# A linear-attention block with a gated feed-forward on one core: the statistics of the last two row tiles a pass sooner, one weight load later, and a finer row of opening products

## The chip, the core and the metric

The kernel runs on one core of a Trainium2 chip. The core has a matrix engine (TensorE, in the profile PE for the products and PEld for the loads of the stationary operand), a vector engine (DVE), a scalar engine (ACT), GpSimd (POOL) and a sync engine (SP) that here only issues DMAs. Every engine works through its own instructions in program order, and semaphores order the engines against each other. The metric is the device time of one execution in microseconds (us), lower is better.

## What is computed

Input x is 2048 rows of 640 numbers in bf16. There are 32 heads of 20 numbers. The reference, cut to what matters:

```python
def _A_ref(x, wqkv, w_phi, wo):                    # linear attention
    q, k, v = split of x @ wqkv into heads
    pq, pk = q @ w_phi[h], k @ w_phi[h]            # per head
    phi_q = concat(softmax(pq), softmax(-pq))
    phi_k = concat(softmax(pk), softmax(-pk))
    kv = sum over rows of phi_k^T v                # per head
    z  = sum over rows of phi_k
    o = (phi_q @ kv) / (phi_q @ z + 1e-6)
    return o @ wo
def _B_ref(x, w_gate, w_up, w_down):
    return (gelu(x @ w_gate) * (x @ w_up)) @ w_down
h   = x + _A_ref(layernorm(x), ...)
out = h + _B_ref(layernorm(h), ...)                # 640 -> 1536 -> 640
```

## The kernel before

The 2048 rows are 16 row tiles t = 0..15 of 128 rows, in four blocks of four tiles. All weights stay in SBUF. The order of the instructions on each engine is the order in which the Python text issues them; nothing reorders them, so a line's place in the text is its place in its engine's queue.

**Opening (L179 to L458).** SP loads x, W_v and the transposed W_k (`load_T(WkT, ...)`). While these are under way TensorE multiplies a constant tile by itself, `warm(*[512] * 7, *[P] * 8)` in L220: 15 products (7 of 512 columns, 8 of 128) whose result nothing reads. Each product in this kernel is a pair of TensorE instructions, a load of the stationary operand (PEld) and the product (PE). Then the first tiles are normalized and transposed by TensorE (`tp`), multiplied by W_v (`pv`), and w_phi is folded into W_k (`fold`, tile `wa`).

**The k pass (L463 to L511), one pass per tile t.** In this order: `k_tile(t)` multiplies tile t by the folded W_k (`pk`, ten products) and ACT writes two exponentials of it (`E`). In some passes `fold` multiplies a part of W_q (`wa`), or `kv_tile` adds phi_k^T v of earlier tiles into the accumulator `kvp` (40 small products per tile: tiles 0, 1 in pass 5; 2 to 5 in pass 9; 6 to 9 in pass 13). Then `v_mm(t + 4)` (`pv`, ten products), `ln_ap(t + 6)`, where ACT writes the normalized tile t + 6 (`ln`) and SP issues the DMA that transposes it into `LN1T`, and `v_ev(t + 4)`, where ACT evicts `pv` into `vS`. Then, in the passes 0, 2, 4 and 6, `ln_st(t + 8, t + 9)` (L485) takes the statistics of two tiles: four `bn_stats` and two `bn_aggr` on DVE (L114, L118), then on POOL variance plus eps (`ve`), its power of -1/2 (`rstd`) and two small scalings (`mr`, L132 to L138). Then `k_norm(t)`: DVE sums `E` (L325) and takes reciprocals (L329), and POOL and DVE write `vt` (L333). At the end of a pass SP may issue a transposing load of a part of W_q (`load_T(WqT, ...)`, passes 7 to 10); at the end of pass 13 it issues the loads of W_o and W_gate (L510, L511: 800 KB and 1920 KB).

**The q groups.** q is made transposed, in 13 groups `QG` of one or two 128x512 tiles: `q_mm(j)` does five products of 512 columns per tile into `pq`, `q_exp(j)` has ACT write two exponentials of it into `Eq[j]`. Pass 15, the last, holds groups 0 to 3: group 0, then `kv_tile` of tiles 10 to 12, then groups 1, 2 and 3. Behind the loop come `kv_tile` of 13 to 15 (L513) and `kv_mask`, where DVE evicts `kvp` into `KV`. Groups 4 and up lie in the text from L752 on, woven with the attention of tiles 0 to 2 (`attn_a`: small products `ab`). `load_late` (L525) loads W_up and W_down after group 4: a POOL copy of one column from `Eq[4]` into `Wu` (L527) makes the DMA behind it on SP (L528) wait for that group, and W_down's two DMAs follow on SP (L530).

**Feed-forward (from L813).** `gate_up` multiplies with W_gate and W_up (`gu`), ACT applies the gelu (`g`), DVE multiplies (`GT`), `down` multiplies with W_down (`pd`); the attention of the tiles 2 to 15 is woven in between. W_gate is first read by the first `gu` product.

PSUM holds four buffers of two banks (`gtile`) until `split`; `kvp` keeps one of them from pass 3 to `kv_mask`.

Of the kernel before, what the change touches and what calls it, by code (L numbers as in the profile page):

```python
# [17 lines left out]
def kernel(  # L18
# [12 lines left out]
    nc = tc.nc  # L31
    P = 128
# [5 lines left out]
    NT = S // P  # L38
# [23 lines left out]
    UH = H // 2  # L62
    QH, QF = H // 4, D // 4
    QUAD = [slice(32 * r, 32 * r + 32) for r in range(4)]

    SLOT = [(c, 3 * c // 2, 2) if c % 2 == 0 else (6 + 3 * (c // 2), 3 * (c // 2) + 1, 3) for c in range(NC)]
    SL = 12
# [16 lines left out]
    Wg = const.tile([P, NC, FF], BF16, name="Wg")  # L84
# [3 lines left out]
    Eq = [const.tile([P, len(g), 2, 512], BF16, name=f"Eq{j}") for j, g in enumerate(QG)]  # L88
# [15 lines left out]
    def gtile(name):  # L104
        return psG.tile([P, 2, 512], F32, name=name, tag="G")

    def ln_stats(pool, tiles, tag, act=True, between=None, log=False):

        n = len(tiles)
        mv = small(pool, [P, n, nc.vector.BN_AGGR_DIM], "mv" + tag)  # L110
        stats = small(pool, [P, n, 2, nc.vector.BN_STATS_DIM], "stats" + tag)
        for j, xt in enumerate(tiles):
            for i in range(2):
                nc.vector.bn_stats(stats[:, j, i, :], xt[:, i * HD:(i + 1) * HD])  # L114
                if between and i == j == 0:
                    between()
        for j in range(n):
            nc.vector.bn_aggr(mv[:, j, :], stats[:, j])  # L118
        ve = small(pool, [P, n], "ve" + tag)
        rstd = small(pool, [P, n], "rstd" + tag)  # L120
        if log is not False:

            def root():
                nc.scalar.activation(ve, mv[:, :, 1], ACTF.Ln, bias=eps)
                nc.scalar.activation(rstd, ve, ACTF.Exp, scale=-0.5)

            if log is True:
                root()
            else:
                log.append(root)  # L130
        else:
            nc.gpsimd.tensor_scalar_add(ve, mv[:, :, 1], EPS)  # L132
            nc.gpsimd.tensor_tensor(rstd, ve, nhalf[:, 0:n], op=ALU.pow)

        mr = small(pool, [P, n], "mr" + tag)
        if act:
            for j in range(n):
                nc.gpsimd.tensor_scalar(mr[:, j:j + 1], mv[:, j, 0:1], rstd[:, j:j + 1], -1.0,  # L138
                                        op0=ALU.mult, op1=ALU.mult)
        return [(xt, mv[:, j, 0:1], rstd[:, j:j + 1], mr[:, j:j + 1]) for j, xt in enumerate(tiles)]  # L140
# [58 lines left out]
    wg_v = B_w_gate.rearrange("(c p) n -> p c n", p=P)  # L199
# [16 lines left out]
    def warm(*cols):  # L216
        for n in cols:
            nc.tensor.matmul(wu[:, 0, 0:n], lhsT=ones[:, 0:P], rhs=ones[:, 0:n], start=True, stop=True)

    warm(*[512] * 7, *[P] * 8)  # L220

    def fold(WT, W2, quarters, ds=range(NC)):


        n, w = (2, QF) if quarters else (1, HD)
        runs = []
        for c in range(NC):
            lo, hi = H0[c] * Dh, (H0[c] + NH[c]) * Dh
            for r in range(2 * n):
                a, b = max(lo, r * w), min(hi, (r + 1) * w)  # L230
                if a < b:
                    runs.append((r // n, r, c, a, b))
        runs.sort()
        for d in ds:
            wa = gtile("wa")
            wr = wa.rearrange("p u (q x) -> p (u q) x", q=n)
            for i, (u, r, c, a, b) in enumerate(runs):
                nc.tensor.matmul(wr[:, r, a - r * w:b - r * w], lhsT=WT[:, c, d * P:(d + 1) * P],  # L238
                                 rhs=BD[:, c].rearrange("p a b -> p (a b)")[:, a - H0[c] * Dh:b - H0[c] * Dh],
                                 start=(i == 0 or runs[i - 1][0] != u),  # L240
                                 stop=(i + 1 == len(runs) or runs[i + 1][0] != u), skip_group_check=True)
            dst, src = W2[:, d, :].rearrange("p (u f) -> p u f", u=2), wr[:, :, 0:w]
            if quarters:
                dst = W2[:, d, :].rearrange("p (c r f) -> p r c f", c=NC, r=4)
                src = src.rearrange("p r (c f) -> p r c f", c=NC)
            if d in (QA if quarters else KA):
                nc.scalar.copy(dst, src)
            else:
                nc.vector.tensor_copy(dst, src)
# [15 lines left out]
    def ln_st(*tiles, act=True, between=None, log=False):  # L265
        for t, v in zip(tiles, ln_stats(p1, [x_sb[t // 4][:, t % 4, :] for t in tiles], "1", act, between, log)):
            lnp[t] = v

    def ln_ap(t, on_act=False, on_pe=False):
        ln = (ln_act if on_act else ln_dve)(p1, "1", *lnp[t])  # L270
        if on_pe:
            lnp[t] = ln
        else:
            transpose_to(LN1T[t // 4][:, :, t % 4 * P:(t % 4 + 1) * P], ln, False)
# [38 lines left out]
    def k_tile(t):  # L313
        pk = gtile("pk")
        proj(pk, t, Wk2, rows=t == 0)
        Ek[t] = ev.tile([P, 2, D], BF16, name="E", bufs=8)
        for s in range(2):
            nc.scalar.activation(Ek[t][:, s, :].rearrange("p (u f) -> p u f", u=2), pk[:, :, 0:HD],  # L318
                                 ACTF.Exp, scale=((lnp[t][2], nrstd[t]) if t in CT else (1.0, -1.0))[s])
# [25 lines left out]
    def kv_tile(t):  # L345

        for s in range(2):
            for c in range(NC):
                i, h, n = SLOT[c]
                for r in range(4):  # L350
                    f0, h0 = r * QF + c * 32, r * QH + h
                    nc.tensor.matmul(kvp[QUAD[r], s * SL + i:s * SL + i + n, :],  # L352
                                     lhsT=Ek[t][:, s, f0:f0 + 32], rhs=Vt[t][:, s, h0:h0 + n, :],
# [23 lines left out]
    def q_exp(j, signs=(0, 1)):  # L377
        for s in signs:
            nc.scalar.activation(Eq[j][:, :, s, :], pqs[j][:, 0:len(QG[j])], ACTF.Exp, scale=(1.0, -1.0)[s])  # L379
# [83 lines left out]
    for t in range(NT):  # L463
        if t == T3:
            kvp = gtile("kvp")[:, 0, 0:2 * SL * VC].rearrange("p (h f) -> p h f", f=VC)
        k_tile(t)
        if t == 0:
            ln_ap(6)
        if t in FQ:
            fold(WqT, Wq2, True, [i for i, f in enumerate(FQ) if f == t])  # L470
        for i in KVG.get(t, ()):
            kv_tile(i)
        for j in range(len(QT)):
            if t == QT[j]:
                q_mm(j)
                q_exp(j)
                for i in KVQ.get(j, ()):
                    kv_tile(i)
        if 0 < t < NT - 4:
            v_mm(t + 4)  # L480
        if t > 0 and t + 6 < NT:
            ln_ap(t + 6, on_act=True)
        if 0 < t < NT - 4:
            v_ev(t + 4)
        if t % 2 == 0 and t + 8 < NT:  # L485
            ln_st(t + 8, t + 9)
        k_norm(t)
        load_T(WqT, 0, *[i for i, f in enumerate(LQ) if f == t])
        if t == 10:
            transpose_to(LN1T[0][:, :, P:2 * P], ln_a(1), False)  # L490
        if t == 12:
            ln_ap(0, on_act=True)
        if t == 7:
            nc.gpsimd.memset(kmask[QUAD[0]], 1.0)
            for k, lo, n, base in ((3, 0, 2, 0), (2, 6, 3, 12)):
                m = kmask[QUAD[0], lo:lo + 6].rearrange("p (k n) -> p k n", k=k)
                nc.gpsimd.affine_select(out=m, in_=m, pattern=[[4, k], [-Dh, n]],
                                        compare_op=ALU.is_ge, fill=0.0, base=base, channel_multiplier=1)
                nc.gpsimd.affine_select(out=m, in_=m, pattern=[[-4, k], [Dh, n]],
                                        compare_op=ALU.is_ge, fill=0.0, base=Dh - 1 - base, channel_multiplier=-1)  # L500
        if t == 8:
            nc.gpsimd.memset(KV, 0.0)
        if t == 9:
            for r in (1, 2, 3):
                nc.sync.dma_start(kmask[QUAD[r]], kmask[QUAD[0]])
        if t == 11:
            nc.gpsimd.tensor_copy(KV[:, 0, :, KC - 1], kmask)
            nc.gpsimd.tensor_copy(KV[:, 1, :, 0], kmask)
        if t == 13:
            nc.sync.dma_start(Wo, wo_v)  # L510
            nc.sync.dma_start(Wg, wg_v)  # L511
    q = len(QT)
    for t in range(13, NT):  # L513
        kv_tile(t)
    kv_mask()
# [28 lines left out]
    def attn_a_mm(t):  # L544
# [9 lines left out]
        for s in range(2):  # L554
            for c in range(NC):
                i, h, n = SLOT[c]
                h += s * QH
                for r, q in enumerate(QUAD):
                    nc.tensor.matmul(ab[r][:, h * KC:(h + n) * KC], lhsT=eq(t, c, s)[q],  # L559
# [295 lines left out]
```

## Time and profile before

| | us |
|---|---|
| median of 3 runs (lowest, highest) | 277.1 (276.02, 277.8) |
| the profiled execution | 276.27 |
| its span, first to last instruction | 274.3 |
| TensorE busy in the span | 268.3 |
| DVE / ACT / POOL busy in the span | 174.2 / 141.0 / 96.3 |

All times inside the trace count from the span's start. The profiled execution's own time is 1.97 us above its span; that remainder lies before the first and after the last instruction. A row of the timeline gives start and length of a group of like instructions, the engine, the line, the operation and its tiles, and in brackets how long the engine had been idle before and what ended that. A matmul's length in the trace includes its latency, so that back-to-back products overlap in it: a 512-column product is listed with 379 ns, and the groups of twenty with 4.32 us, 0.216 us from start to start. "PEq", "SPq" and the like are an engine's sequencer, that is its instruction stream. "issue" means that the engine waited for nothing that the profile shows. In the part on the DMA queues q1 is the queue of the kernel's own DMAs, and q8 and q14 carry instructions.

### The profile page before, as it was taken

The page shows a single profiled execution, that of the slowest core. Times are in us where ns is not written, and L with a number is a line of the kernel's source. Part 1 is how long each engine was busy: PE and PEld are TensorE (multiplying, and loading weights), DVE is VectorE, ACT ScalarE, POOL GpSimd, SP SyncE. Part 2 cuts the span into 40 slices and gives each one's busy share as a digit, 9 for nine tenths or more (in the row PEclk, how much of TensorE's full clock was granted, in tenths as well). Part 3 has the DMA queues.
Part 4 walks back from the last instruction along what each step waited for, and adds up shares of the span by engine and source line. Part 5 has one row for each costly group of instructions (what it writes and reads, how often), then busy time and mean ns, then how long its engine had stood idle before and what let it go on. Part 6 is the DMA issues. An engine that isn't in the chain of part 4 may idle for free.

```text
span 274.3 us, 7230 instructions
## 1 busy us (share of the span) xinstructions
PE 268.3 (98%) x2978; PEld 171.8 (63%) x2995; DVE 174.2 (63%) x332; ACT 141.0 (51%) x241; POOL 96.3 (35%) x219
## 2 busy tenths in 40 slices
PE   8999999999999999999999999999999999999996
PEld 4777777764555887788754555675555576444574
DVE  5889999997585776775459863336976333333332
ACT  5789888786689755374534445212445510223100
POOL 4248899675002227374221552101165300000000
PEclk9999999999999999999999999999999999999999
DMA  7962527578078022323111232110214211000011
GB/s 204 215 225 56 75 51 98 75 149 312 2 264 310 5 50 43 79 54 71 38 38 49 26 72 50 45 53 1 68 30 62 37 48 50 24 0 0 2 48 48
DMA packets 42400, 21.46 MB, mean 78 GB/s; under 512 B 35200, under 2 KB 40576, under 8 KB 42368
## 3 DMA queue, kind: packets, MB, share of 16 engines
q1 hardware_dynamic: 41712, 20.98, 31.2%
q8 instruction: 23, 0.38, 0.6%
q10 hardware_dynamic: 656, 0.03, 0.2%
q14 instruction: 9, 0.07, 0.1%
HBM read 10.18 MB, written 2.62 MB: 47 GB/s over the span
## 4 chain that ended last, share of the span: by engine, by line
PE 90%; DMA 3%; ACT 2%; issue 1%; POOL 1%; DVE 1%; SPq 0%; ACTq 0%
PE gu L691 38%; PE pd L710 19%; PE po L631 8%; PE pq L374 8%; PE pk L285 6%; PE pv L285 5%; PE ab L559 2%; PE kvp L352 2%; DMA LN1T<-ln 2%; DMA Wv<-in_A_wqkv_dram 1%; PE wa L238 1%; ACT vS L305 1%; ACT ln L144 1%; PE tp L157 1%; PE pv L301 1%
## 5 line engine op out<-in xcount | busy, mean ns | idle before, releaser
L697 DVE TENSOR_TENSOR GT<-gu,g 128x512 bf16<-128x512 f32 (+1 forms) x60 | 34.5, 581 | 47.3 <-PE gu L691 38.5
L694 ACT ACTIVATE g<-gu 128x512 bf16<-128x512 f32 (+1 forms) x60 | 30.7, 512 | 63.7 <-PE gu L691 62.8
L691 PE MATMUL gu<-LN2T,Wg 128*128 128x512 bf16 (+1 forms) x289 | 61.2, 335 | 0.6
L691 PE MATMUL gu<-LN2T,Wu 128*128 128x512 bf16 (+1 forms) x300 | 61.7, 336 | 0.0
L710 PE MATMUL pd<-Wd,GT 128*128 128x320 bf16 (+2 forms) x396 | 53.5, 295 | 0.0
L710 PEld LDWEIGHTS <-GT 128*128 128x128 bf16 x396 | 37.9, 98 | 14.6 <-DVE GT L697 0.2
L691 PEld LDWEIGHTS <-Wu 128*128 128x128 bf16 x300 | 29.3, 98 | 22.6
L691 PEld LDWEIGHTS <-Wg 128*128 128x128 bf16 x300 | 28.6, 98 | 20.8
L285 PEld LDWEIGHTS <-LN1T 128*128 128x128 bf16 x290 | 27.8, 98 | 10.8 <-DMA LN1T<-ln 0.4
L713 DVE TENSOR_TENSOR y<-pd,x_sb 128x320 bf16<-128x320 f32 (+2 forms) x29 | 13.9, 480 | 29.4 <-PE pd L710 29.4
L333 POOL TENSOR_TENSOR vt<-vS,rs 128x672 bf16<-128x672 bf16 x22 | 29.2, 1346 | 7.6 <-DVE rs L329 7.2
L631 PE MATMUL po<-Wo,oT 128*128 128x320 bf16 x160 | 24.4, 299 | 0.0
L374 PE MATMUL pq<-LN1T,Wq 128*128 128x512 bf16 x94 | 23.1, 379 | 1.2 <-PE kvp L352 0.5
L285 PE MATMUL pk<-Wk,LN1T 128*128 128x320 bf16 x160 | 24.2, 299 | 0.0
L325 DVE TENSOR_REDUCE sk<-E 128x64 f32<-128x1280 bf16 x16 | 22.9, 1430 | 0.0
L379 ACT ACTIVATE Eq<-pq 128x1024 bf16<-128x1024 f32 (+1 forms) x26 | 20.0, 828 | 3.8 <-PE pq L374 3.8
L285 PE MATMUL pv<-Wv,LN1T 128*128 128x320 bf16 x130 | 19.8, 299 | 0.2 <-DMA LN1T<-ln 0.2
L631 PEld LDWEIGHTS <-oT 128*128 128x128 bf16 x160 | 15.5, 98 | 7.0 <-ACT oT L158 0.5
L318 ACT ACTIVATE E<-pk 128x640 bf16<-128x640 f32 x28 | 18.2, 706 | 3.1 <-PE pk L285 3.0
L608 DVE TENSOR_TENSOR tt<-AB,w 128x1280 bf16<-128x1280 f32 x12 | 17.8, 1485 | 1.0 <-POOL w L601 0.9
L144 ACT ACTIVATE ln<-x_sb,v,rstd 128x640 bf16<-128x640 bf16 x14 | 12.9, 920 | 10.7 <-POOL v L670 10.3
L374 PEld LDWEIGHTS <-Wq 128*128 128x128 bf16 x100 | 9.4, 98 | 10.7 <-issue 1.1
(114 smaller groups left out, 288.6 us busy)
## 6 DMA issues: line engine op xcount, KB each, us to landing
out_dram<-y SPq DMA_DIRECT2D x15, 160.0 KB, 1.8
Wg<-in_B_w_gate_dram SPq DMA_DIRECT2D x1, 1920.0 KB, 10.7
Wu<-in_B_w_up_dram SPq DMA_DIRECT2D x1, 1920.0 KB, 8.7
Wd<-in_B_w_down_dram SPq DMA_DIRECT2D x2, 960.0 KB, 12.0
x_sb<-in_A_x_dram SPq DMA_DIRECT2D x2, 640.0 KB, 6.3
Wo<-in_A_wo_dram SPq DMA_DIRECT2D x1, 800.0 KB, 5.0
x_sb<-in_A_x_dram SPq DMA_DIRECT2D x4, 160.0 KB, 3.4
Wv<-in_A_wqkv_dram SPq DMA_DIRECT2D x2, 320.0 KB, 4.3
```

The source lines that it names most:

```text
L285: nc.tensor.matmul(ps[:, u, 0:HD], lhsT=lnT(t, c), rhs=W[:, c, u * HD:(u + 1) * HD], start=(c == 0), stop=(c == NC - 1))
L318: nc.scalar.activation(Ek[t][:, s, :].rearrange("p (u f) -> p u f", u=2), pk[:, :, 0:HD], ACTF.Exp, scale=((lnp[t][2], nrstd[t]) if t in C ...
L325: nc.vector.reduce_sum(sk, Ek[t].rearrange("p s (h f) -> p (s h) f", f=Dh), axis=AX.X)
L333: eng.tensor_tensor(vt[:, s], vS[t % 8], rs[:, s * H:(s + 1) * H, None].to_broadcast([P, H, VC]), ALU.mult)
L374: nc.tensor.matmul(pqs[j][:, i, :], lhsT=Wq2[:, kc, c * P:(c + 1) * P], rhs=LN1T[b][:, kc, :], start=(kc == 0), stop=(kc == NC - 1))
L379: nc.scalar.activation(Eq[j][:, :, s, :], pqs[j][:, 0:len(QG[j])], ACTF.Exp, scale=(1.0, -1.0)[s])
L608: nc.vector.tensor_tensor(tt.rearrange("p s (h f) -> p s h f", f=Dh), num, w[:, :, :, None].to_broadcast([P, 2, H, Dh]), ALU.mult)
L631: nc.tensor.matmul(pos[u], lhsT=st[t][:, c, :], rhs=Wo[:, c, u * HD:(u + 1) * HD], start=(c == 0), stop=(c == NC - 1))
L691: nc.tensor.matmul(gu[i][:, 0:n], lhsT=W[:, c, f * P:(f + 1) * P], rhs=LN2T[b][:, c, a0:a1], start=(c == 0), stop=(c == NC - 1))
L694: nc.scalar.activation(g[:, 0:n], gu[0][:, 0:n], ACTF.Gelu_apprx_tanh)
L697: nc.vector.tensor_tensor(st[b, "g", f][:, a0:a1], gu[1][:, 0:n], g[:, 0:n], ALU.mult)
L710: nc.tensor.matmul(ps, lhsT=st[b, "g", f][:, tl * P:(tl + 1) * P], rhs=Wd[:, f, f0:f1], start=(f == 0), stop=(f == NF - 1))
```

## The change

Three edits. The dictionary `ST` replaces the rule of L485: the statistics are taken in passes 0, 2, 4 and 5 instead of 0, 2, 4 and 6, so tiles 14 and 15 come one pass earlier. The load of W_gate moves from the end of pass 13 to behind the loop, and a POOL copy of one column from `Eq[2]` (the third q group, second exponential) into `Wg` makes it wait for that group. The opening is 20 products in place of 15; the columns are 5 x 512 + 256 + 14 x 128 = 4608 and were 7 x 512 + 8 x 128 = 4608.

```diff
+    ST = {0: (8, 9), 2: (10, 11), 4: (12, 13), 5: (14, 15)}
...
-    warm(*[512] * 7, *[P] * 8)
+    warm(*[512] * 5, 256, *[P] * 14)
...
-        if t % 2 == 0 and t + 8 < NT:
-            ln_st(t + 8, t + 9)
+        if t in ST:
+            ln_st(*ST[t])
...
         if t == 13:
             nc.sync.dma_start(Wo, wo_v)
-            nc.sync.dma_start(Wg, wg_v)
     q = len(QT)
+    nc.gpsimd.tensor_copy(Wg[:, 0, 0:1], Eq[q - 2][:, 0, 1, 0:1])
+    nc.sync.dma_start(Wg, wg_v)
     for t in range(13, NT):
         kv_tile(t)
```

## The prediction

> **What bounds the kernel now.** I read the page's busy times first, then who made TensorE wait, then the timeline around each of those waits.
>
> ```profile
> PE 268.3 (98%) x2978; PEld 171.8 (63%) x2995; DVE 174.2 (63%) x332; ACT 141.0 (51%) x241; POOL 96.3 (35%) x219
> ```
>
> TensorE is busy for 268.3 of the 274.3 us. Its work is not changed (the opening has the same columns), so what can be won is its idle time, 6.0 us at the most. The waits view for PE:
>
> ```profile
> PE pq L374 <- PE kvp L352: 0.5, 1, 0.5
> PE pq L374 <- issue: 0.4, 1, 0.4
> PE pv L301 <- DMA Wv<-in_A_wqkv_dram: 0.3, 1, 0.3
> PE pv L285 <- DMA LN1T<-ln: 0.2, 1, 0.2
> ```
>
> Four waits behind the first instruction. The third lies in the opening, where no edit moves W_v. I measure the others by starts, since listed matmul lengths contain latency. The timeline around them, in time order:
>
> ```profile
> 46.07 0.50 PE L238 MATMUL wa<-BD,WqT 128*128 128x140 bf16 x8
> 46.81 0.31 PE L285 MATMUL pv<-Wv,LN1T 128*128 128x320 bf16 x1 [0.25 <-DMA LN1T<-ln]
> 49.54 0.50 PE L238 MATMUL wa<-BD,WqT 128*128 128x140 bf16 x8
> 49.88 0.30 PE L285 MATMUL pv<-Wv,LN1T 128*128 128x320 bf16 x1
> 61.60 1.14 PE L352 MATMUL kvp<-vt,E 128*32 128x42 bf16 x120
> 62.67 0.39 PE L374 MATMUL pq<-LN1T,Wq 128*128 128x512 bf16 x1
> 65.70 0.81 PE L374 MATMUL pq<-LN1T,Wq 128*128 128x512 bf16 x3
> 66.88 0.59 PE L374 MATMUL pq<-LN1T,Wq 128*128 128x512 bf16 x2 [0.36 <-issue]
> 68.69 1.14 PE L352 MATMUL kvp<-vt,E 128*32 128x42 bf16 x120
> 70.33 0.38 PE L374 MATMUL pq<-LN1T,Wq 128*128 128x512 bf16 x1 [0.50 <-PE kvp L352]
> 157.58 4.32 PE gu L691 x20
> ```
>
> *First stall.* From the fold to pv it is 49.88 - 49.54 = 0.34 us in pass 11 and 46.81 - 46.07 = 0.74 in pass 10: 0.40 lost, waiting for the transposed tile 14. *Second.* The last row (from the chain of waits) gives 4.32 / 20 = 0.216 from one 512-column product to the next. Three start from 65.70, so the last at 66.13, and the next only at 66.88: 0.74 - 0.22 = 0.53 lost in the middle of group 2, "issue". *Third.* From the 120 kvp products to pq it is 62.67 - 61.60 = 1.07 once and 70.33 - 68.69 = 1.64 the second time: 0.57 lost. Together 1.50 us.
>
> The second and third look unlike each other in the list, but a count joins them. Here are the page's instruction queue, the table of stretches, and the DMA queues' view for 59.3 to 64.3 (first row), 64.3 to 65.5, 67.8 to 69.0 and 72.0 to 73.4 us:
>
> ```profile
> q8 instruction: 23, 0.38, 0.6%
> ...
> 66.87:70.32 3.45, 2.96 (x128) 1.81 (x128) 0.37 (x2) 2.71 (x5) 1.00 (x1) 1.00 0.06 23
> 77.70:88.00 10.30, 10.25 (x69) 5.73 (x68) 7.73 (x16) 9.55 (x14) 1.59 (x4) 1.00 1.02 371
> ...
> q1 hardware_dynamic: 938, 1.71, 93.4%
> ...
> q8 instruction: 1, 0.02, 5.4%
> ...
> q8 instruction: 1, 0.02, 5.1%
> ...
> q8 instruction: 1, 0.02, 5.9%
> ```
>
> q8 moved 23 packets for TensorE's 2978 + 2995 = 5973 instructions, 260 each, and between the ends of the two stalls lie 128 + 128 = 256 instructions. So I read both as TensorE out of instructions: it reached the end of a block of 256 before the packet with the next was in. The packet of the first stall moved within 64.3 to 65.5 and TensorE went on at 66.88; that of the second within 67.8 to 69.0, and it went on at 70.33: both 1.3 to 1.4 us behind the end of the stretch. With nothing else on the DMA engines, a block that began at 66.88 called a packet that moved from 67.8 on, and its instructions ran at 70.33: 3.45 us from call to use. The packet before that was called by 61.65 at the latest (the block before 66.88 begins just inside the 61.60 kvp products, whose 120 pairs nearly fill it) but moved only after 64.3: no q8 packet moved in 59.3 to 64.3, while W_o and W_gate held the engines at 93%. That lateness I charge to W_gate.
>
> The Trainium skill, page "Runtime: NRT & Kernel Launch", section "Instruction fetch mechanics", says that instructions are refilled in 16 KiB blocks of 256 and that the cost of crossing a block is mostly hidden. The trace agrees with the 256 and not with the hiding: 0.53 + 0.57 us show.
>
> **Part one, the statistics.** Rows of the trace around pass 6:
>
> ```profile
> 35.30 3.86 POOL L333 TENSOR_TENSOR vt<-vS,rs 128x672 bf16<-128x672 bf16 x3 [0.18 <-DVE rs L329]
> 35.13 1.43 DVE L325 TENSOR_REDUCE sk<-E 128x64 f32<-128x1280 bf16 x1
> 37.13 1.61 DVE L114 BATCH_NORM_STATS2 stats<-x_sb 128x6 f32<-128x320 bf16 x4
> 40.35 1.11 POOL L138 TENSOR_SCALAR mr<-mv,rstd 128x1 f32<-128x1 f32 x2
> 41.27 0.92 ACT L144 ACTIVATE ln<-x_sb,mr,rstd 128x640 bf16<-128x640 bf16 x1 [0.85 <-POOL mr L138]
> 42.21 1.21 SPq L160 DMA_TRANSPOSE LN1T<-ln  x1
> q8 instruction: 1, 0.02, 5.3%
> DMA to landing us min/median/max: 2.6/2.6/3.5
> ```
>
> ACT is free at 41.27 - 0.85 = 40.42 and waits for mr until 41.27. A pass sooner, the statistics stand on DVE ahead of pass 5's sum and reciprocal, at 35.13 instead of 37.13, so 2.0 us earlier. POOL has two of its three vt to do first (2 x 1.29 = 2.6, from 35.30 to 37.9); its small steps for the statistics now begin right behind the third vt, at 39.2, so all of them move by one vt, 1.3 us, and the first mr, which releases ACT at 41.27, is there at 40.0, before ACT asks. So ln of tile 14 starts 0.85 sooner, and its transpose is issued at 41.36. What it displaces: pass 5's sum and reciprocal end 2.0 us later on DVE, and the third vt on POOL waits for them, until about 41. Its reader is the last of the four tiles in pass 9's kvp, which pass here at about 43; the sum of pass 6 starts where it did, since DVE does the same work in between. On SP nothing is passed. I cost this at nothing; without the 2 us of cover it would cost up to 2.0.
>
> Is 0.85 enough for 0.40? The transpose landed late: 2.6 us is its median and 3.5 its worst, and an instruction packet (the q8 row, view for 43.3 to 44.9) crossed it. Moved 0.85 forward it is mostly through by 43.3. Sooner by 0.85 alone covers 0.40; missing the packet gives 0.9 more. If the packet still catches it, the gain here is nothing. I take 0.40; ends 0 and 0.40. Next late after tile 14 would be tile 15 at 49.88, which has no wait now.
>
> **Part two, W_gate.**
>
> ```profile
> 58.46 0.51 SPq L511 DMA_DIRECT2D Wg<-in_B_w_gate_dram  x1
> 67.72 2.92 ACT L379 ACTIVATE Eq<-pq 128x1024 bf16<-128x1024 f32 x4 [0.74 <-PE pq L374]
> 75.19 0.77 POOL L527 COPY Wu<-Eq 128x1 bf16<-128x1 bf16 x1 [7.32 <-ACT Eq L379]
> 75.98 0.37 SPq L528 DMA_DIRECT2D Wu<-in_B_w_up_dram  x1
> 89.73 0.72 PE L691 MATMUL gu<-LN2T,Wg 128*128 128x256 bf16 x5
> ```
>
> Added: a POOL copy (0.77 by the like one for Wu), and a wait of POOL and then SP for Eq[2]. Behind the copy on POOL stands only the copy for Wu, before which POOL idles 7.32 us; on SP only Wu's DMA at 75.98. Both cost nothing. Eq[2] is complete with the second of the four exponentials at 67.72, about 69.7; copy and 0.51 of issue make 70.9. The load takes some 5 us (1920 KB at the 371 GB/s of the stretch from 77.7, when Wu and Wd fill the engines, is 5.3), begins moving some 1.8 us after issue as Wu's did (75.98 to 77.7), and ends near 77 to 78: 12 us ahead of 89.73, and about when Wu's bytes begin. If it ran into Wu's, Wu and Wd would end by some 1 us later than 88.0; Wu is read within 1 us of 89.73, so that is the cover.
>
> What it gives: the engines are free from about 62 (W_o alone, 800 KB, 2.2 us). The packet called by 61.65 is then usable by 61.65 + 3.45 = 65.1, and it was needed at 66.35: the second stall goes. The block after it is called 0.5 us sooner or more. Ends for this stall: 0 (the load was not the cause) and 0.53; I take 0.53.
>
> **Part three, 20 products.** The columns are the same 4608.
>
> ```profile
> 0.83 4.00 PE L218 MATMUL wu<-const-bfloat16-1.0 128*128 128x512 bf16 x15 [0.83 <-PEq L839]
> 3.77 0.79 PEld L218 LDWEIGHTS <-const-bfloat16-1.0 128*128 128x128 bf16 x7 [0.28 <-issue]
> 4.94 0.89 PE L157 MATMUL tp<-ident,xc 128*128 128x128 bf16 x10
> 6.33 1.79 PE L301 MATMUL pv<-Wv,LN1T 128*128 128x320 bf16 x12 [0.27 <-DMA Wv<-in_A_wqkv_dram]
> ```
>
> Seven of the small ones take 0.79, 0.11 us a pair; that is their column time, so finer cutting costs nothing: end at 4.83 as before, ahead of tp at 4.94. Were each of the 14 dearer by 0.04, tp would slip 0.5 and the 0.27 in front of pv would hide half. What does change is the count: 5 pairs, 10 instructions, so every later block of 256 begins 10 instructions earlier in the work. In group 2 that is 5 products, 1.08 us: the block of the second stall is needed at 65.27 instead of 66.35 (usable by 65.1: just), and the block after it is called that much sooner. That one is then needed 10 instructions before the end of kvp at 69.8 and usable by 65.3 + 3.45 = 68.7, so the third stall goes too. Ends: 0 and 0.57; I take 0.57, as the call also gains by part two.
>
> **Sum.** 0.40 + 0.53 + 0.57 = 1.50 us. TensorE has no such wait after 71, so it reaches the end: 276.27 - 1.50 = 274.77 for the profiled execution. That one lies 0.8 under the median of 277.1; against the median it is 275.6, my figure.
>
> **The rivals.** *One of the three stays.* For it: the margins of 0.2 us for the block at 65.27 and of a few tenths for the transpose; against: calls may come well before the crossing I bound them by. The gain is 0.93 to 1.10: 276.1.
>
> *The loads did not hold the packets up.* Then both blocks starve as before, only part one pays: -0.40, 276.7. For it: the third packet, at 72.0, moved 1.7 us after 70.33 with nothing else on the engines, so calls vary by themselves. Against: 64.3 is 2.7 us after the latest call. The Trainium skill, page "DMA: Bandwidth & Descriptors", section "Queues, rings and completion order", speaks for it: a DMA engine takes turns between its queues packet by packet, by which a waiting instruction packet is passed by one packet and not by a whole load.
>
> *Slower: the shifted packets hit other transposes.* Every later instruction packet moves 5 product pairs sooner, up to 1.08 us in the q groups and almost nothing in the kvp runs, while the transposes stay with ACT's and DVE's work. A hit costs a transpose 0.9 us (3.5 against 2.6), and TensorE what of that is not slack. Place: the products at 46.81 and 49.88, which start as soon as their fold lets them, and their like in earlier passes. For it: the one hit that the trace shows on TensorE's path came about in just this way. Against: the waits view has one such wait in the whole k pass. It decides from two hits without slack on, since 1.50 must be eaten: 277.1 - 1.50 + 1.80 = 277.4; five would be over 1%.
>
> **How the numbers follow.** 1% of 277.1 is 2.8 us, about what a measurement here can tell from no change. Forecast 0.58 (275.6), one stall stays 0.20 (276.1), loads innocent 0.13 (276.7), slower 0.09 (277.4 and up). The forecast's own range is 274.6 to 276.6, from the runs' spread of 276.02 to 277.8. For 8 in 10 I take in the next two cases and leave out what is beyond: 274.4 to 277.2. Faster by over 1% would need 274.3: 0.06. Slower by over 1%: 0.04. Within: 0.90.
>
> **What would show it.** Right: pv of tile 14 starts 0.34 after its fold's start, ln of tile 14 with no wait on mr; no "issue" gap inside group 2; kvp to pq 1.07 in both places; W_gate's bytes in 71 to 78. Wrong: an idle TensorE 10 instructions before the old places, a gu that waits for Wg or Wu, or new waits for a transposed tile.

## The result, and the profile after

| | us |
|---|---|
| changed kernel, median of 22 runs (lowest, highest) | 275.63 (275.06, 276.54) |
| kernel before, median of 22 runs beside them | 276.27 (275.39, 277.8) |
| ratio, 95% interval | 0.9976 [0.9965, 0.9988] |
| profiled execution after, its span | 275.48, 273.4 |
| profiled execution before, its span | 276.27, 274.3 |

The change is a small gain: 0.64 us, within 1%. My figure of 275.6 us fell on the measured 275.63, but not for the reason I gave. I took 1.50 us off a median of three runs, 277.1, and that median lay 0.83 us above the median of 22. The gain in the sum was more than twice the real one, and the high median covered it: that the figure fits is luck. The rest of this text is about the 0.86 us that I promised and that did not come.

All three stalls that the prediction named are gone. The page's busy line and the waits view for PE, after:

```profile
PE 268.0 (98%) x2983; PEld 172.0 (63%) x3000; DVE 174.5 (64%) x332; ACT 141.1 (52%) x241; POOL 96.0 (35%) x220
```

```profile
PE wu L220 <- PEq L842: 0.8, 1, 0.8
PE pv L303 <- DMA Wv<-in_A_wqkv_dram: 0.8, 1, 0.8
```

Of the four waits quoted before, only the opening's wait for W_v is left, and it is longer (0.8 against 0.3). The timeline after, in time order, at the places of the prediction:

```profile
6.77 0.43 PE L303 MATMUL pv<-Wv,LN1T 128*128 128x320 bf16 x2 [0.75 <-DMA Wv<-in_A_wqkv_dram]
...
35.20 1.52 PE L287 MATMUL pk<-Wk,LN1T 128*128 128x320 bf16 x10
36.86 0.72 PE L287 MATMUL pv<-Wv,LN1T 128*128 128x320 bf16 x4
...
36.85 0.52 PEld L287 LDWEIGHTS <-LN1T 128*128 128x128 bf16 x5 [0.47 <-DMA LN1T<-ln]
...
40.97 0.92 ACT L146 ACTIVATE ln<-x_sb,mr,rstd 128x640 bf16<-128x640 bf16 x1
...
46.76 0.50 PE L240 MATMUL wa<-BD,WqT 128*128 128x140 bf16 x8
47.10 0.57 PE L287 MATMUL pv<-Wv,LN1T 128*128 128x320 bf16 x3
...
61.75 1.14 PE L354 MATMUL kvp<-vt,E 128*32 128x42 bf16 x120
62.82 5.57 PE L376 MATMUL pq<-LN1T,Wq 128*128 128x512 bf16 x24
68.32 1.14 PE L354 MATMUL kvp<-vt,E 128*32 128x42 bf16 x120
69.39 0.82 PE L376 MATMUL pq<-LN1T,Wq 128*128 128x512 bf16 x2
...
69.35 0.19 POOL L514 COPY Wg<-Eq 128x1 bf16<-128x1 bf16 x1 [1.27 <-ACT Eq L381]
...
69.57 0.38 SPq L515 DMA_DIRECT2D Wg<-in_B_w_gate_dram  x1
```

What the reader is to see. The normalization of tile 14 (40.97) no longer waits for `mr`, and `pv` follows the fold by 47.10 - 46.76 = 0.34 us. The q products behind the first kvp run are one unbroken group of 5.57 us, with no "issue" (24 are listed, but the length holds 25 starts at 0.216; one record is missing). From kvp to pq it is 62.82 - 61.75 = 1.07 and 69.39 - 68.32 = 1.07. W_gate's copy takes 0.19 us where I wrote 0.77 by the row of W_up's copy. Its bytes move for the most part from 72 to 77, at 375 GB/s in the windows table:

```profile
72.00:77.00 5.00, 4.89 (x62) 2.33 (x62) 3.88 (x11) 4.06 (x5) 0.77 (x1) 1.00 1.06 375
```

The instruction packet that before moved only after 64.3 us now moves in 61.7 to 62.9, in the DMA queues' view of after:

```profile
q8 instruction: 1, 0.02, 5.2%
```

But two things were given back. The first `pv` starts at 6.77 instead of 6.33, because W_v landed later. And `pv` of tile 11 starts 36.86 - 35.20 = 1.66 us behind its ten pk products, where the same place before shows 36.20 - 34.84 = 1.36, in the timeline of the kernel before:

```profile
34.84 1.52 PE L285 MATMUL pk<-Wk,LN1T 128*128 128x320 bf16 x10
36.20 0.98 PE L285 MATMUL pv<-Wv,LN1T 128*128 128x320 bf16 x6
```

To see where all of it went I cut the span of each profile at the starts of fixed products: the first `pv`, the first kvp product of the five runs of `kv_tile` (k1 tiles 0 and 1, k2 tiles 2 to 5, k3 6 to 9, k4 10 to 12, k5 13 to 15), and the first `ab`. The numbers are differences of starts in the trace, in us; "first pv" counts from the span's start; pv to k1 is 23.56 to 23.63 in all but one profile (g_only 23.98), and k3 to k4 is 6.77 to 6.90 in all.

| kernel (parts in it, opening) | first pv | k1 to k2 | k2 to k3 | k4 to k5 | k5 to ab |
|---|---|---|---|---|---|
| before (none, 15) | 6.33 | 11.83 | 12.98 | 7.09 | 2.81 |
| after (1 + 2 + 3, 20) | 6.77 | 12.05 | 12.59 | 6.57 | 2.28 |
| s_only (1, 15) | 6.58 | 11.87 | 12.54 | 6.57 | 3.03 |
| g_only (2, 15) | 6.54 | 11.89 | 13.26 | 6.57 | 2.28 |
| g2 (2, 15) | 6.76 | 11.73 | 12.74 | 6.57 | 2.28 |
| w_only (3, 20) | 6.63 | 11.73 | 12.75 | 8.08 | 2.28 |
| gw (2 + 3, 20) | 6.63 | 11.94 | 12.74 | 6.70 | 2.28 |
| gw2 (2 + 3, 20) | 6.48 | 12.07 | 12.55 | 6.57 | 2.28 |
| sg (1 + 2, 15) | 6.47 | 11.73 | 12.57 | 6.57 | 2.28 |
| sg2 (1 + 2, 15) | 6.46 | 11.74 | 12.56 | 6.57 | 2.28 |
| sg17 (1 + 2, 17) | 6.67 | 12.16 | 12.55 | 6.57 | 2.28 |
| sgw_again (1 + 2 + 3, 20) | 6.69 | 11.73 | 12.57 | 6.57 | 2.28 |
| sgw2 (1 + 2 + 3, 20) | 6.42 | 12.33 | 12.58 | 6.57 | 2.28 |
| sg_shift (1 + 2, 15, ten instructions added) | 6.51 | 12.49 | 12.59 | 6.57 | 2.28 |

After against before: +0.44 (first pv), +0.22, -0.39, -0.12 (k3 to k4), -0.52, -0.53, together -0.90, the difference of the two spans. The first stall lies in k2 to k3, the second in k4 to k5, the third in k5 to ab.

### The profile page after: what moved, and what is told of

Read it like the earlier page. It is cut to its first block, busy times and chain, and to the rows that moved or that the text cites. A ratio compares the mean times of both kernels' runs of the same rounds, so it can differ in the third digit from the quotient of the medians.

```text
span 273.4 us, 7242 instructions
## 1 busy us (share of the span) xinstructions
PE 268.0 (98%) x2983; PEld 172.0 (63%) x3000; DVE 174.5 (64%) x332; ACT 141.1 (52%) x241; POOL 96.0 (35%) x220
## 4 chain that ended last, share of the span: by engine, by line
PE 94%; DMA 3%; ACT 1%; issue 1%; DVE 1%; SPq 0%
PE gu L694 38%; PE pd L713 19%; PE po L634 8%; PE pq L376 8%; PE pk L287 7%; PE pv L287 6%; PE ab L562 2%; PE kvp L354 2%; DMA Wv<-in_A_wqkv_dram 2%; DMA LN1T<-ln 2%; PE wa L240 1%; PE tp L159 1%; PE pv L303 1%; ACT vS L307 1%; DVE LN1T L160 0%
```

## The experiments

After the result two things were open. One: do the second and third stall come from instruction blocks that W_gate's load makes late (my theory), or do the blocks come late by themselves, with the loads innocent and the shift by part three doing the work (the rival)? Two: what gave back the gain: the finer opening, the shifted blocks that land on transposes, or chance? Each part was run alone, then in pairs. Each group of runs was made on one chip beside the kernel before. Its medians were 276.27 us (s_only, g_only, w_only, gw), 275.86 (sg, sg17, sgw_again), 276.09 (g2, gw2, sg2, sgw2) and 276.15 (sg_shift); each median below is over 12 runs.

**Part one alone (s_only).**

```diff
+    ST = {0: (8, 9), 2: (10, 11), 4: (12, 13), 5: (14, 15)}
...
-        if t % 2 == 0 and t + 8 < NT:
-            ln_st(t + 8, t + 9)
+        if t in ST:
+            ln_st(*ST[t])
```

> Part one alone: statistics of tiles 14 and 15 in pass 5, nothing else. Theory A (the stall at pv of tile 14 came from its late transpose): ln of tile 14 no longer waits for mr, pv starts 0.34 us after its fold, the gap of 0.53 us inside group 2 and the 0.57 us behind kvp stay; 0.40 us less, ratio 0.9986. Rival (the transpose is late because an instruction packet crosses it, whenever it starts): wait and time unchanged, ratio 1.000.

Measured: 275.86 us, ratio 0.9983 [0.9969, 0.9997]. The stall of tile 14 is gone (k2 to k3 12.54). In the timeline of this profile the third stall is still there:

```profile
68.04 1.14 PE L354 MATMUL kvp<-vt,E 128*32 128x42 bf16 x120
69.89 1.24 PE L376 MATMUL pq<-LN1T,Wq 128*128 128x512 bf16 x5 [0.72 <-PE kvp L354]
```

It is 69.89 - 68.04 - 1.07 = 0.78 us, while the second stall is missing (k4 to k5 6.57) with W_gate still early. So with the load early a block is late by an amount that varies; in this execution the packet for the block of the second stall moved at 63.56, in that of before at 64.36. Here that was just in time, but the packet after it moved only at 67.31, 3.75 us later, and that was too late. In all fourteen profiles this next packet moves 3.35 to 3.98 us behind the one before it (starts in the trace), so it passes its lateness on.

**Part two alone (g_only, and once more as g2).**

```diff
-            nc.sync.dma_start(Wg, wg_v)
...
+    nc.gpsimd.tensor_copy(Wg[:, 0, 0:1], Eq[q - 2][:, 0, 1, 0:1])
+    nc.sync.dma_start(Wg, wg_v)
```

> Part two alone: W_gate behind the third q group. Theory A (TensorE ran out of instructions because the packet waited behind the W_o and W_gate loads): the q8 packet that moved at 64.4 us moves by 62.5, the gap inside group 2 goes, the gap behind kvp shrinks or goes since its block is called sooner; 0.5 to 1.1 us less, ratio 0.996 to 0.998. Rival (the loads are innocent; the gap is a wait for a PSUM buffer or the packets vary by themselves): both gaps stay, ratio 1.000.

> Two by two on one chip, always with part two: this one has neither part one nor part three. Theory B (the three stalls go with parts one and two alone; 20 products only add, by packets onto the transpose of tile 11, a thin margin in group 2 and perhaps a later first pv): second of the four or level with the changed kernel, ratio 0.9965. Rival (the parts' order on the first chip was chance): all four level, 0.997 to 0.998.

Measured: g_only 275.4 us, 0.9963 [0.9951, 0.9975]; g2 275.34 us, 0.9973 [0.9947, 0.9998]; by the medians 0.87 and 0.75 us under before. The timeline of g_only:

```profile
46.62 0.50 PE L238 MATMUL wa<-BD,WqT 128*128 128x140 bf16 x8
47.77 0.31 PE L285 MATMUL pv<-Wv,LN1T 128*128 128x320 bf16 x1 [0.65 <-DMA LN1T<-ln]
...
62.44 1.14 PE L352 MATMUL kvp<-vt,E 128*32 128x42 bf16 x120
63.51 5.57 PE L374 MATMUL pq<-LN1T,Wq 128*128 128x512 bf16 x25
69.01 1.14 PE L352 MATMUL kvp<-vt,E 128*32 128x42 bf16 x120
70.08 1.04 PE L374 MATMUL pq<-LN1T,Wq 128*128 128x512 bf16 x4
```

Both stalls of the q groups are gone with the old opening: 25 products without a break, and 1.07 us twice. That is the first thing I had wrong, since I had put the third stall to part three. The stall of tile 14 is still there, as it should be, and in this execution it is 47.77 - 46.62 - 0.34 = 0.81 instead of 0.40.

**Part three alone (w_only).**

```diff
-    warm(*[512] * 7, *[P] * 8)
+    warm(*[512] * 5, 256, *[P] * 14)
```

> Part three alone: 20 opening products in the same 4608 columns. Theory A (blocks of 256 instructions): the gap inside group 2 moves five products forward and, with W_gate still in the way, grows from 0.53 to about 1.6 us, the gap behind kvp goes: some 0.5 us more, ratio 1.002. Rival 1 (gaps have nothing to do with blocks): gaps where they were, ratio 1.000. Rival 2 (the finer opening delays the first pv, which began 0.44 us later in the changed kernel's profile): first pv near 6.8 instead of 6.3 us, ratio 1.0016 from that alone.

Measured: 276.75 us, ratio 1.0017 [1.0002, 1.0032], so this part by itself does not help. Its timeline:

```profile
62.63 2.76 PE L374 MATMUL pq<-LN1T,Wq 128*128 128x512 bf16 x12
66.75 2.97 PE L374 MATMUL pq<-LN1T,Wq 128*128 128x512 bf16 x13 [1.35 <-issue]
69.64 1.14 PE L352 MATMUL kvp<-vt,E 128*32 128x42 bf16 x120
70.71 0.39 PE L374 MATMUL pq<-LN1T,Wq 128*128 128x512 bf16 x1
```

The break in group 2 now comes behind 12 products of this stretch; before it came behind 17 (62.67 to 66.35 at 0.216). Five products are ten instructions, the shift by which every block begins earlier. And it has grown: the 13th product was due at 62.63 + 12 x 0.216 = 65.22 and started at 66.75, 1.53 us late, since the block was needed 1.08 us sooner and its packet came hardly sooner (it moved at 64.19, before at 64.36). This run is what shows that the stall in group 2 sits on a block of instructions and not on a place in the work. The table gives the run's loss its place: k4 to k5 is 0.99 longer than before and k5 to ab 0.53 shorter.

**Parts two and three (gw, and once more as gw2).** The edits of g_only and w_only together:

```diff
-    warm(*[512] * 7, *[P] * 8)
+    warm(*[512] * 5, 256, *[P] * 14)
...
-            nc.sync.dma_start(Wg, wg_v)
...
+    nc.gpsimd.tensor_copy(Wg[:, 0, 0:1], Eq[q - 2][:, 0, 1, 0:1])
+    nc.sync.dma_start(Wg, wg_v)
```

> Parts two and three without part one. Theory A: no gap inside group 2 nor behind kvp (1.10 us less), the wait of pv of tile 14 stays at 0.4; ratio 0.996. If the opening (20 products) costs 0.44 us by itself: 0.9977, and first pv near 6.8 us. Rival (a packet five products sooner hits the transpose of tile 11, as in the changed kernel's profile at 36.9 us, 0.30 us): the same wait shows here, since part one has no say in it.

> Parts two and three. Theory B: the slowest of the four, 0.9985, 0.3 to 0.6 us over part two alone; first pv near 6.6 to 6.7, packet of the third block at 33.5. Rival: level with the others.

Measured: gw 276.06 us, 0.9991 [0.9976, 1.0006]; gw2 275.76 us, 0.9978 [0.9959, 0.9998]. Part three added to part two makes it 0.66 us dearer (276.06 against 275.4) and 0.42 dearer (275.76 against 275.34) on the same chips. gw came out above either figure that I had given for it (0.996 and 0.9977). Its profile keeps 0.13 us of the stall in group 2 (k4 to k5 6.70): the packet moved at 63.11, although W_gate was late; W_o's last data packet ended at 63.16 there. In gw2's profile k1 to k2 is 12.07 us, as after.

**Parts one and two, the old opening (sg, and once more as sg2).** The changed kernel, with one line back as it was before:

```diff
-    warm(*[512] * 5, 256, *[P] * 14)
+    warm(*[512] * 7, *[P] * 8)
```

> Parts one and two with the old opening of 15 products. Theory A (the 20 products are what costs: they bring the packet of the third block forward from 35.0 to 33.5 us, onto the transpose of tile 11): the gains of part one alone (0.47) and part two alone (1.02) add up, ratio 0.9946, and pv of tile 11 waits for nothing. Rival (parts one and two win the same time, or the gains are eaten elsewhere): no better than part two alone, ratio 0.996 to 0.998.

> Parts one and two. Theory B: the fastest of the four, 0.9950, 0.4 us under part two alone; profile without any wait of TensorE from the first pv to the end. Rival: level with the others.

Measured: sg 274.97 us, 0.9973 [0.9958, 0.9987]; sg2 275.04 us, 0.9956 [0.9936, 0.9976]. By its ratio sg falls in the rival's range and not on the theory's 0.9946, sg2 comes near the theory's 0.9950; against part two alone on the same chip sg2 is 0.30 lower, with overlapping intervals. The waits view for PE in sg holds two waits, both in the opening:

```profile
PE wu L220 <- PEq L842: 0.8, 1, 0.8
PE pv L303 <- DMA Wv<-in_A_wqkv_dram: 0.4, 1, 0.4
```

**The changed kernel beside them (sgw_again, and once more as sgw2).** This is the whole change again, as a pair to sg and sg2. What it has over these is the line:

```diff
-    warm(*[512] * 7, *[P] * 8)
+    warm(*[512] * 5, 256, *[P] * 14)
```

> The changed kernel once more, on the chip of the two runs before it. Ratio 0.9976 as measured; its profile shows the packet of the third block at 33.4 to 33.7 us and pv of tile 11 waiting 0.2 to 0.3 us (theory A), or, if that wait was chance, none.

> All three parts. Theory B: 0.2 to 0.5 us over parts one and two, 0.9975; packet of the third block at 33.5, pv of tile 11 with or without a wait of up to 0.3, as the packet ends late or early. Rival: level with the others.

Measured: sgw_again 275.16 us, 0.998 [0.997, 0.9991], 0.19 above sg; sgw2 275.61 us, 0.9986 [0.9965, 1.0007], 0.57 above sg2. The intervals overlap in each pair. But over the five pairs on equal chips with and without part three (w_only against before, gw against g_only, gw2 against g2, and these two) the kernel with part three is the dearer each time: +0.48, +0.66, +0.42, +0.19, +0.57. w_only's interval lies above 1 and those of gw and g_only do not overlap; in the other three pairs they do. The first of the five is the stall that grew in group 2, not a hit on a transpose. sgw_again's profile shows no wait at tile 11 (k1 to k2 11.73): the transpose landed 3.5 us after issue there, so a hit doesn't reach TensorE in every execution. In sgw2's the wait is at tile 9, whose transpose took 4.5 us with the second block's packet at 28.64, in the timeline:

```profile
31.31 0.45 PE L287 MATMUL pv<-Wv,LN1T 128*128 128x320 bf16 x2 [0.50 <-DMA LN1T<-ln]
```

**Seventeen opening products (sg17).** On top of sg:

```diff
-    warm(*[512] * 7, *[P] * 8)
+    warm(*[512] * 6, 256, *[P] * 10)
```

> As the run before, with 17 opening products in the same 4608 columns (6 of 512, one of 256, 10 of 128). Two products more are enough to put the end of the third block from pv of tile 11 into pk of tile 7, before the wait that held the packet back. Theory A: packet at about 33.5 us, transpose of tile 11 hit, pv of tile 11 waits 0.2 to 0.3 us; group 2 has a larger margin than with 20; ratio 0.9955. Rival (20 products cost in the opening or at group 2, in proportion to their number): packet at 35 us, no wait at tile 11, ratio as with 15 products or 0.1 us above.

Measured: 275.04 us, 0.9968 [0.9953, 0.9983], 0.07 above sg. Its profile has waits for transposed tiles too (k1 to k2 12.16). The third block's packet did not move to 33.5 as expected; it moved at 34.66, in sg at 34.87, and yet the transpose of tile 11 took 4.3 us. The time says nothing about two more products.

**The old opening, but ten instructions more (sg_shift).** Is it the finer cutting that costs, or the shift? On top of sg, five constant products more in the second row of them, whose result nothing reads either:

```diff
-    warm(*[P] * 4)
+    warm(*[P] * 9)
```

> Parts one and two with the old opening, and five more zero products of 128 columns in the second row of them (9 for 4), where TensorE waits for W_v anyway: ten more instructions ahead of everything, without the finer opening. Theory B (the end of the blocks is what 20 products change): packet of the third block at 33.4 to 33.7 us instead of 35, transpose of tile 11 hit, waits at pv of tile 9 or 11 in some executions, 0.2 to 0.5 us over parts one and two, ratio 0.997. Rival (the finer cutting of the opening is what costs): packet at 35, ratio 0.9955.

Measured: 275.42 us, 0.9974 [0.9956, 0.9991]. Against a before of 276.15 that is a gain of 0.73, less than sg's 0.89 and 1.05, but on another chip and within the spread: the time decides nothing here. The profile does. In sg the third instruction packet moves from 34.87 us on, when the transpose of tile 11 is nearly through; in sg_shift from 33.52 on, while it is under way. The timeline of sg, its DMA queues' row for 34.7 to 36.2, and from the view of the transposing line the landing of this one transpose, issued at 32.27:

```profile
34.89 1.52 PE L287 MATMUL pk<-Wk,LN1T 128*128 128x320 bf16 x10
36.24 1.39 PE L287 MATMUL pv<-Wv,LN1T 128*128 128x320 bf16 x9
```

```profile
q8 instruction: 1, 0.02, 4.1%
```

```profile
DMA to landing us min/median/max: 2.9/2.9/2.9
```

The same of sg_shift, the queues' row for 33.4 to 34.7, the transpose issued at 32.31:

```profile
35.06 1.52 PE L287 MATMUL pk<-Wk,LN1T 128*128 128x320 bf16 x10
37.03 0.58 PE L287 MATMUL pv<-Wv,LN1T 128*128 128x320 bf16 x3 [0.44 <-DMA LN1T<-ln]
```

```profile
q8 instruction: 1, 0.02, 5.7%
```

```profile
DMA to landing us min/median/max: 4.7/4.7/4.7
```

In sg `pv` follows `pk` by 36.24 - 34.89 = 1.35 us; in sg_shift by 37.03 - 35.06 = 1.97. The transpose took 4.7 us instead of 2.9 and TensorE lost 0.62 of it. The opening of 20 products has the same signature, in the views of after for 33.4 to 34.7 and for the same transpose, issued at 32.58:

```profile
q8 instruction: 1, 0.02, 7.1%
```

```profile
DMA to landing us min/median/max: 4.2/4.2/4.2
```

There TensorE lost 1.66 - 1.35 = 0.31. Both agree on one margin: 4.7 - 0.62 = 4.1 and 4.2 - 0.31 = 3.9, so the tile may land about 4 us after issue and nothing is lost. The hit needs the shift, not the finer cutting. All profiles together say the same: this transpose landed 2.6 to 3.3 us after issue in the six with the old number of TensorE instructions, and 3.5 to 4.7 in the eight with four or ten more. The 1.8 us of sg_shift need not all come from this packet, as a packet of another engine's instructions (q14) crossed the transpose as well, for 1.53 us from 34.20; in sg one of 0.60 us at 33.51 left it at 2.9.

## Why the prediction was right and wrong

*The diagnosis: right.* All three stalls were where I put them and all three went. That the second is the end of a block is shown by w_only, where ten instructions moved the break by exactly five products. For the third no run shows it so directly: it lies 256 instructions behind the second, and its packet follows the second's. One reading under it was wrong: 3.45 us is not the time from the call of a packet, at the start of a block, to its use. In sg the next packet moved at 64.94, 0.9 us before TensorE reached the end of the block in group 2 (62.18 + 17 x 0.216 = 65.85), so the call lies ahead of that.

*Part one, 0.40: right.* The reasoning held (no wait for `mr`, 0.34 from fold to pv, no new wait of TensorE in sg). The term was one execution's: in the six profiles without this part k2 to k3 is 12.55 to 13.26, 12.84 in the mean, and in the eight with it 12.54 to 12.59, so 0.27 on average.

*Part two, 0.53: right cause, too small.* It was worth about 1.05 in the profiles: 7.09 to 6.57 and 2.81 to 2.28, in g_only and in g2, with no other edit; by the medians 0.87 and 0.75. The packet for the block in group 2 moved at 63.56 to 64.36 us in the three profiles with W_gate early and at 61.12 to 63.11 in the eleven with it late (starts of the packets in the trace). Against this stands the rule that I had weighed (the Trainium skill, page "DMA: Bandwidth & Descriptors", section "Queues, rings and completion order": turns between queues, packet by packet). Taken alone it would not have let the packet be late by 2 us, and the trace does not show a packet that passes a load so easily. With W_gate late it moved at the end of W_o's load in each of the eleven profiles, at most 0.7 us before the last data packet was through, also in gw, where that was latest; with W_gate early it moved 0.5 to 2.1 us after that end, while W_gate's packets were under way. That points to a packet that waits behind loads, not to a later call, but no run varied the load alone against a fixed call, so it stays open. The rival of the innocent loads is out.

*Part three, 0.57: this is the step that failed.* I wrote "Ends: 0 and 0.57; I take 0.57, as the call also gains by part two". The call gained by part two alone, and I had the means to see it: once the block of group 2 is in time, the next is called that much sooner, the very sentence that stands at the end of part two ("The block after it is called 0.5 us sooner or more"). What the runs showed in its place: with the old opening the third stall goes too (2.28 in g_only and g2, as in after), since the next packet follows the one before by its 3.35 to 3.98 us, late or not. I booked the same cause twice, under two edits, when one was enough. Part three's measured worth is not above zero: the medians with it are 0.19 to 0.66 us higher in the five pairs, of which three overlap in their intervals.

*Part three's price: named, and placed outside the forecast.* That "finer cutting costs nothing" holds: the first pv lies at 6.33 to 6.76 with 15 products (six profiles, mean 6.52) and at 6.42 to 6.77 with 20 (six, mean 6.60). What the profiles show as a cost is the shift of the blocks. That was my rival "the shifted packets hit other transposes", with 0.09 as its chance; it came in a small form, together with the forecast. I had put it at the products behind the folds of passes 10 and 11 and at their like in earlier passes; it came only in earlier ones, at tiles 9 and 11, in k1 to k2. I had 0.9 us per hit; the transpose lost 1.3 and 1.8 against 2.9, of which 0.31 and 0.62 reached TensorE. One hit did not make the kernel slower, as I had reckoned. By the profiles k1 to k2 is 11.80 in the mean of the six with 15 products and 11.98 in that of the six with 20, a price of 0.18; with the 0.08 of the first pv it makes 0.26, and the pairs of medians say 0.46 on average. The rest I can't place.

*The sum.* For the profiled execution I had 274.77; it was 275.48, 0.71 more. Part two brought 1.05 where parts two and three together were to bring 1.10, part one 0.39. What was missing was the first pv, +0.44, and the hit, within the +0.22 of k1 to k2; and the execution's own time fell by 0.79 where its span fell by 0.90. The first pv lies within the spread just given for either opening, and 6.33 in before is the earliest of all fourteen profiles. In the medians the three stalls were worth less than in the one execution that I measured them in: without part three, sg and sg2 gained 0.89 and 1.05 where I had 1.50. For the median I used three runs where the figure moved by 0.83 with 22, more than the gain to be found. From 276.27, the profiled execution and also the median of 22, the same sum gives 274.77, 0.86 too low.

The best version found is parts one and two with the old opening: 274.97 us beside a before of 275.86, and 275.04 beside 276.09. It was below the changed kernel both times, by 0.19 and 0.57, though each pair's intervals overlap.

## What to carry to other kernels

When two stalls share a cause, follow the second through the cure of the first before crediting it to another edit: a block of instructions that arrives in time calls the next one sooner. Where TensorE runs many short products, count 256 of its instructions from one unexplained "issue" gap to the next, and keep big loads away from there. Any edit that adds or removes TensorE instructions moves all later blocks, so look at which transposes their packets then fall on, and drop such an edit when its own gain is not shown.

## What the runs showed of the hardware

One instruction packet can hold up a whole transpose. The q8 rows above are shares of 16 engines: the packet took 0.057 x 16 x 1.3 = 1.2 us in sg_shift and 0.071 x 16 x 1.3 = 1.5 us in after, and the transpose landed 1.8 and 1.3 us later than in sg (4.7 and 4.2 against 2.9), in sg_shift with the q14 packet beside it. I had reckoned with 0.9.

Crossing a block of 256 instructions is free or dear by what else moves: in group 2 nothing in ten profiles with W_gate late and 0.13 us in the eleventh (gw), 0.53 us before, and 1.53 us in w_only. The Trainium skill, page "Runtime: NRT & Kernel Launch", section "Instruction fetch mechanics", calls it "mostly hidden"; the trace agrees with that in group 2 where W_gate's load is out of the way, and does not in two of the three profiles where its 1920 KB are on the way (before and w_only), nor at the block behind a late one (0.57 us before, 0.78 in s_only).
